# A fused attention and gated-MLP kernel: wide query weights, earlier bias and spatial loads, normalization in one step, first loads on two queues

## The chip, the core and the metric

The kernel runs on one core of a Trainium2 chip. The core has five engines that work through their own instruction lists: TensorE (PE in the profile; PEld is its weight load), VectorE (DVE), ScalarE (ACT), GpSimd (POOL) and SyncE (SP). SP, ACT and POOL can also issue transfers (DMAs) between memory and the core; an issue by POOL takes POOL's own time. The metric is the device time of one launch in microseconds (us), as the median of several runs. A second figure is the profiled execution: one launch with the hardware profiler, from which every duration in this document comes.

## What is computed

Inputs are q, k, v of shape 8 batches x 8 heads x 576 tokens x 64, a feature matrix w_phi (64 x 128) and the weights of a gated MLP. Cut to what matters:

```python
def phi(x):                                   # per head
    proj = x @ w_phi                          # 64 -> 128 features
    proj = proj - max(abs(proj), axis=-1)
    return concat([exp(proj), exp(-proj)])
q_p, k_p = phi(q), phi(k)
kv  = einsum('bhsf,bhsd->bhfd', k_p, v);  z = k_p.sum(tokens)
x   = (q_p @ kv) / (q_p @ z + 1e-6)           # heads side by side: 8 x 576 x 512

h = relu(x @ w_in)                            # 512 -> 1024
u, v = h[..., :512], h[..., 512:]
v_n = (v - mean(v)) / sqrt(var(v) + 1e-6)
v_s = einsum('ts,bsd->btd', w_spatial, v_n) + b_spatial[:, None]
out = (u * v_s) @ w_out                       # 512 -> 512
```

All inputs and the output are float32; the matrix products run in bfloat16.

## The kernel before

**Units.** The attention part (stage A) runs over 36 units, numbered in the order in which they are worked. A "pair" unit is one pair of heads of one batch with its first 512 tokens as four blocks of 128. The last 64 tokens of the eight heads of two batches make one "tail" unit. Units 0, 1, 3, 4 are batch 0, unit 2 is the tail of batches 0 and 1, units 5 to 8 are batch 1, unit 9 is the tail of batches 2 and 3, units 10 to 13 are batch 2, and so on.

**Steps.** `step(i)` (line 636) walks a fixed list of phases. In step i the keys and queries of unit i are projected (`by_token`, L267), their largest magnitudes taken on DVE (L279 for keys, L293 for queries), the key features made on ACT (`kf`, L282) and V scaled by the key factors `em` on POOL (`vs`, L307; for tails `vst`, L322). One step later the query maxima, split into two bfloat16 parts by POOL (`mhl`, L296/297, by DVE for the first five units), are transposed by PE (`a_max_t`, L328). Two steps later (a step more or less for the first five units) come the query features (`qf`, L366) and the sums over tokens (L379 to L384), three later the numerator (L399) and four later the transposed result `xT`. So PE's order of work is fixed when the program is built, whatever is ready.

**Projection with the maximum.** For batches 0 and 1 the query maximum is subtracted by a second matrix product with `sel` (L353, L360). From batch 2 on (`merged`) it is folded into the weights: `wm` holds for even heads the weights with selection rows in partitions 64 to 79 and for odd heads the other half plus the selection (`weights_with_max`, L239 to L243, twelve POOL instructions in steps 6 and 7). There the query operand also takes the maxima as extra rows: `q_even` copies half of the transposed queries by a DMA, and DVE writes the maxima (L331, L332).

**Loads.** Batch 0's first heads come as float32 by SP and are cast by DVE (heads 0, 1) and POOL (heads 2, 3, and the tails). All later q and k are cast on the way by DMAs that POOL issues (`load`, `load_tail`); v comes by SP (`load_v`). From batch 2 on, q and k are transposed by DMAs issued by SP (`cross`, three steps before use), which wait there for the load. The table `io` (L676 to L712) says after which step each load is issued.

**The MLP (stage B).** When a batch's `xT` is complete, its tasks (`b_tasks`, L592) join a queue, and `fill` puts them between the phases of later steps: `b_v` (L448, relu on ACT L450, mean and variance on DVE L451/L452), `b_root` (L454 to L462), `b_ln` (L465: normalization into `vn` on POOL), `b_u` (L503, L505), `b_s` (L524, L525 with the transposed spatial weights `w_spT`, multiplied into `uT` by DVE at L527) and `b_o` (L549, copied out at L552, stored by SP at L558). The tail of each batch has the same steps (`b_v_tail` and the like); its normalized rows go to `vnt`. The bias is one extra row of `w_spT`, multiplied by a row of ones in `vnt`.

`root` makes both the factor and the shift of the normalization from the variance and the mean, in four POOL instructions:

```python
var = var + 1e-6                      # L458
rs0 = var ** -0.5                     # L459
rs1 = -(mean * rs0)                   # L460, L461
vn  = vr * rs0 + rs1                  # L465, normalize
```

**Spatial weights.** `w_spatial` is loaded in three parts (`wsp`, `wspr`, `wspt`), transposed by PE between tasks of batch 0 (`transpose_spatial`, L210) and copied into `w_spT` by DVE. The same function has ACT write the two bias rows (L230 to L233).

Of the kernel before, what the change touches and what calls it, by code (L numbers as in the profile page):

```python
# [8 lines left out]
FP32 = mybir.dt.float32  # L9
BF16 = mybir.dt.bfloat16  # L10
# [6 lines left out]
def kernel(  # L17
# [106 lines left out]
    for i in range(2):  # L124
        nc.scalar.dma_start(out=wphi_f[i * D:(i + 1) * D, :], in_=w_phi)
    alloc(0)
    first = {}
    for h0 in (0, 2):
        for x, t in (("k", k), ("q", q)):
            first[x, h0] = s2.tile([P, 2, NB * D], FP32, tag="ob", name="first", bufs=6)  # L130
            pin(nc.sync.dma_start)(out=first[x, h0], in_=main_ap(t, 0, h0, 2))
    alloc_tail(0)
    tails = ld.tile([P, H * NB, D], FP32, tag="v_f", name="tails")
    for n, t in enumerate((k, q)):
        for i in range(2):
            pin(nc.sync.dma_start)(out=tails[i * TL:(i + 1) * TL, n * H:(n + 1) * H, :], in_=tail_ap(t, i))
# [5 lines left out]
    zero = cpool.tile([P, 1], BF16)  # L142
    pin(nc.vector.memset)(zero, 0.0)
# [25 lines left out]
    pin(nc.vector.memset)(vst[1], 0.0)  # L169
# [7 lines left out]
    pin(nc.scalar.copy)(out=vst[0].rearrange("p b s h d -> p (b s h d)"), in_=zero.to_broadcast([P, 4 * H * DA]))  # L177
# [3 lines left out]
    for i in range(2):  # L181
        fill_vnt(i, nc.gpsimd.tensor_copy)
    for x in ("k", "q"):
        pin(nc.gpsimd.tensor_copy)(out=half_tile(x, 0, 0)[:, 2:4], in_=first[x, 2])
    load("k", 0, 1, 0, 2)
    load("q", 0, 1, 0, 2)
# [7 lines left out]
    wsp = s2.tile([P, NB, T0], BF16, tag="vn", name="wsp", bufs=2)  # L194
    wspr = cpool.tile([P, NB, TL], BF16)
    wspt = s2.tile([TL, S], BF16, tag="ob", name="wspt", bufs=6)
    bsp_row = s2.tile([P, S], FP32, tag="xT", name="bsp_row", bufs=3)
    nc.sync.dma_start(out=bsp_row[TL:TL + 1, :], in_=moe_b_spatial)
    nc.sync.dma_start(out=bsp_row[0:1, :], in_=moe_b_spatial)
# [10 lines left out]
    def transpose_spatial(i):  # L210

        pt = psum.tile([P, S], BF16, tag="bank", name="pt")
        if i < NB:
            sc = POS[i]
            for tp, c in enumerate(POS):
                nc.tensor.transpose(out=pt[:, tp * P:(tp + 1) * P], in_=wsp[:, c, bass.ds(sc, P, step=NB)],
                                    identity=ident)
            nc.tensor.transpose(out=pt[:, T0:S], in_=wspt[:, bass.ds(sc, P, step=NB)],
                                identity=ident[:TL, :TL])
            nc.vector.tensor_copy(out=w_spT[:, i, :], in_=pt)  # L220
            return
        for bl in range(2):
            lo = bl * TL
            for tp, c in enumerate(POS):
                nc.tensor.transpose(out=pt[lo:lo + TL, tp * P:(tp + 1) * P], in_=wspr[:, c, :], identity=ident)
            nc.tensor.transpose(out=pt[lo:lo + TL, T0:S], in_=wspt[:, T0:S], identity=ident[:TL, :TL])
            nc.vector.tensor_copy(out=w_spT[lo:lo + TL, NB + bl, :], in_=pt[lo:lo + TL, :])
        for bl, row in ((0, TL), (1, 0)):
            r = slice(row, row + 1)
            pin(nc.scalar.copy)(  # L230
                out=w_spT[r, NB + bl, 0:T0].rearrange("o (a b p) -> o a b p", a=2, b=2),
                in_=bsp_row[r, 0:T0].rearrange("o (p b a) -> o a b p", a=2, b=2))
            pin(nc.scalar.copy)(out=w_spT[r, NB + bl, T0:S], in_=bsp_row[r, T0:S])  # L233


    def merged(u):
        return u["pair"] and u["b"] >= XB

    def weights_with_max(n):  # L239
        for j in range(4 * n, 4 * n + 4, 2):  # L240
            pin(nc.gpsimd.tensor_copy)(out=wm[:, j, :], in_=wphi2[:, 0:F])
            pin(nc.gpsimd.tensor_tensor)(out=wm[:, j + 1, :], in0=wphi2[:, F:2 * F], in1=sel[:, j + 1, :], op=ALU.add)
            pin(nc.gpsimd.tensor_copy)(out=wm[D:D + 2 * H, j, :], in_=sel[0:2 * H, j, :])  # L243
# [210 lines left out]
    def root(mv, r, n):  # L454

        var = small.tile([P, NB, 1], FP32, tag="var", name="var")
        rs = small.tile([P, NB, 2], FP32, tag="rs", name="rs")
        nc.gpsimd.tensor_scalar(out=var[r, 0:n], in0=mv[r, 0:n, 1:2], scalar1=1e-6, scalar2=None, op0=ALU.add)  # L458
        nc.gpsimd.tensor_tensor(out=rs[r, 0:n, 0:1], in0=var[r, 0:n], in1=neghalf[r, 0:n].unsqueeze(2), op=ALU.pow)  # L459
        nc.gpsimd.tensor_tensor(out=var[r, 0:n], in0=mv[r, 0:n, 0:1], in1=rs[r, 0:n, 0:1], op=ALU.mult)  # L460
        nc.gpsimd.tensor_scalar(out=rs[r, 0:n, 1:2], in0=var[r, 0:n], scalar1=-1.0, scalar2=None, op0=ALU.mult)  # L461
        return rs  # L462

    def normalize(dst, src, rs):
        nc.gpsimd.tensor_scalar(out=dst, in0=src, scalar1=rs[:, 0:1], scalar2=rs[:, 1:2],  # L465
                                op0=ALU.mult, op1=ALU.add)

    def b_v(b, j):
        d = st[b]
        if j == 0:  # L470
            d["vn"] = s2.tile([P, NB, HALF], BF16, tag="vn", name="vn", bufs=2)
            d["mv"] = small.tile([P, NB, 2], FP32, tag="mv", name="mv")
            d["vr"] = {}
        d["vr"][j] = s2.tile([P, HALF], BF16, tag="vr", name="vr", bufs=5)
        stats = small.tile([P, 6], FP32, tag="stats", name="stats")
        v_mm(lambda kc: d["xT"][:, kc, j * P:(j + 1) * P], d["vr"][j], slice(0, P), stats, d["mv"][:, j, :])

    def b_root(b):
        st[b]["rs"] = root(st[b]["mv"], slice(0, P), NB)

    def b_ln(b, j):
        d = st[b]
        normalize(d["vn"][:, j, :], d["vr"][j], d["rs"][:, j, :])

    def b_v_tail(g, bls):
# [6 lines left out]
        rstd = root(mv, r, 1)  # L492
        for bl in bls:
            r = slice(bl * TL, (bl + 1) * TL)
            normalize(vnt[g % 2][r, bl, :], vr[r], rstd[r, 0, :])
# [96 lines left out]
    def b_tasks(b):  # L592
# [8 lines left out]
        ts.append((0.0, lambda: b_root(b)))  # L601
# [79 lines left out]
    at(1, load_v, 1)  # L681
    at(2, load, "k", 1, 0)
    at(2, load, "q", 1, 0)
    at(3, load, "k", 1, 1)
    at(3, load, "q", 1, 1)
    at(4, load_weight, w_in_bf[:, :, HALF:DFF], cols[:, :, HALF:DFF])
    at(4, load_weight, wspt, moe_w_spatial[T0:S, :])
    at(5, tail_scale, 0, 1)
    at(5, load_weight, wsp, rows[:, :, 0:T0])
    at(5, load_weight, wspr, rows[:, :, T0:S])  # L690
    at(6, load_weight, w_in_bf[:, :, 0:HALF], cols[:, :, 0:HALF])
    at(8, load_weight, w_out_bf, moe_w_out.rearrange("(kc p) f -> p kc f", p=P))
    for u in units:
        i = u["i"]
        if not u["pair"] and u["g"] > 0:
            early = 1 if u["g"] > 1 else 0
            at(i - AT - early, load_tail, "k", u["g"])
            for x in ("q", "v"):
                at(i - AT + 1 - early, load_tail, x, u["g"])
        if u["pair"] and u["b"] >= XB:  # L700
            if u["pj"] == 0:
                for n, (x, y) in enumerate((("k", 0), ("q", 0), ("k", 1), ("q", 1))):
                    at((4, 4, 6, 7)[n] if u["b"] == XB else i - AB + n, load, x, u["b"], y)
# [4 lines left out]
    at(6, weights_with_max, 0)  # L708
    at(7, weights_with_max, 1)
# [39 lines left out]
```

## Time and profile before

| | us |
|---|---|
| median of 3 runs | 285.23 (282.81 to 285.92) |
| profiled execution | 284.76 |
| its span, first to last instruction | 282.7 |

Busy time of each engine over the span, from the page:

| engine | busy us | share |
|---|---|---|
| PE | 257.1 | 91% |
| DVE | 231.2 | 82% |
| ACT | 219.5 | 78% |
| POOL | 200.5 | 71% |

The granted TensorE clock of the execution was 0.986 of full speed. In the profile's lists of waits, "POOL vs L307 <- ACT em L302: 17.6, 9, 4.0" means that POOL's instruction that writes vs at line 307 stood waiting for ACT's em of line 302, 17.6 us in all, nine times, 4.0 us at the longest. A wait is only put down when the engine had nothing else to do, as each engine takes its list in order. A DMA's "us to landing" counts from its issue until its data are there. Lines that say L61 are recorded through a helper (`pin`) that keeps an instruction at its place in the program's order.

### The profile page before, as it was taken

The numbers are of one execution on the slowest core, as the hardware profiler recorded it, in microseconds if no ns is written. First come the engines' busy times: TensorE is split into PE (matmuls) and PEld (weight loads), VectorE is DVE, ScalarE is ACT, GpSimd is POOL, SyncE is SP. The second block draws the span as 40 slices with busy tenths as digits, with TensorE's granted clock in tenths as the row PEclk, the third lists the DMA queues.
The fourth block names the chain that finished last, engine by engine and source line by source line (L and its number), as shares of the span: only waits on it lengthen the run. The fifth ranks groups of instructions, "written<-read, shape, count | busy, mean of one in ns | idle before, by whom it ended". The sixth has DMA issues, their size and how long they took to land.

```text
span 282.7 us, 8134 instructions
## 1 busy us (share of the span) xinstructions
PE 257.1 (91%) x3001; PEld 173.1 (61%) x3042; DVE 231.2 (82%) x576; ACT 219.5 (78%) x499; POOL 200.5 (71%) x362
## 2 busy tenths in 40 slices
PE   2777979986999999999999999999999999999993
PEld 1466866754776667666666775766666765654441
DVE  7979987875799979998889989998889897566341
ACT  5689996978399997899889987899699977723601
POOL 5988999999859886799949974889548832511710
PEclk9979999999799999999999999999999999999999
DMA  7989999999986999989989999999766301120305
GB/s 205 238 205 125 152 144 217 111 164 195 225 87 163 130 243 196 162 206 210 214 96 130 207 252 138 200 214 217 86 122 132 86 2 68 46 77 37 112 3 186
DMA packets 85148, 42.43 MB, mean 150 GB/s; under 512 B 52146, under 2 KB 80498, under 8 KB 85108
## 3 DMA queue, kind: packets, MB, share of 16 engines
q1 hardware_dynamic: 60020, 30.95, 55.0%
q0 software_dynamic: 24928, 10.89, 34.9%
q8 instruction: 24, 0.39, 0.6%
q14 instruction: 16, 0.13, 0.2%
q10 hardware_dynamic: 160, 0.07, 0.1%
HBM read 32.85 MB, written 9.44 MB: 150 GB/s over the span
## 4 chain that ended last, share of the span: by engine, by line
PE 62%; POOL 12%; ACT 9%; DVE 6%; DMA 4%; issue 4%; SPq 0%; POOLq 0%; ACTq 0%; DVEq 0%
PE ps L524 9%; PE pv L448 9%; PE po L549 9%; PE ps L267 6%; PE pu L503 6%; ACT kf L282 5%; PE pv L379 4%; PE pn L399 4%; PE pq L345 3%; DMA q_bf<-in_q_dram 3%; PE ps L525 2%; POOL vs L307 2%; POOL vst L61 2%; DVE stats L451 2%; ACT qf L366 2%
## 5 line engine op out<-in xcount | busy, mean ns | idle before, releaser
L282 ACT ACTIVATE kf<-ps 128x512 bf16<-128x512 f32 x144 | 76.2, 637 | 9.9 <-DVE mk L279 9.5
L307 POOL TENSOR_TENSOR vs<-v_f,em 128x512 bf16<-128x512 f32 x64 | 65.5, 1044 | 19.0 <-ACT em L302 17.6
L366 ACT ACTIVATE qf<-pq 128x512 bf16<-128x512 f32 x128 | 66.6, 620 | 9.6 <-PE pq L345 8.5
L279 DVE TENSOR_REDUCE mk<-ps 128x4 f32<-128x512 f32 x72 | 47.7, 677 | 1.2 <-PE ps L267 0.5
L293 DVE TENSOR_REDUCE mq<-ps 128x4 f32<-128x512 f32 x62 | 39.8, 680 | 2.6 <-PE ps L267 1.4
L524 PE MATMUL ps<-w_spT,vn 128*128 128x512 bf16 x116 | 33.1, 384 | 3.6 <-POOL vn L465 3.1
L527 DVE TENSOR_TENSOR uT<-ps,uT 128x512 bf16<-128x512 f32 x32 | 22.0, 687 | 16.8 <-PE ps L525 16.8
L451 DVE BATCH_NORM_STATS2 stats<-vr 128x6 f32<-128x512 bf16 (+1 forms) x40 | 26.7, 684 | 7.3 <-ACT vr L450 6.9
L549 PE MATMUL po<-w_out_bf,uT 128*128 128x512 bf16 x121 | 32.0, 380 | 0.4
L503 PE MATMUL pu<-xT,w_in_bf 128*128 128x512 bf16 x121 | 31.5, 380 | 0.5 <-issue 0.2
L448 PE MATMUL pv<-w_in_bf,xT 128*128 128x512 bf16 x116 | 30.7, 380 | 0.7
L450 ACT ACTIVATE vr<-pv 128x512 bf16<-128x512 f32 (+1 forms) x40 | 23.5, 615 | 7.6 <-PE pv L448 5.9
L379 PE MATMUL pv<-vs,kf 128*128 128x66 bf16 x512 | 24.3, 194 | 1.3 <-ACT kf L282 1.3
L390 DVE TENSOR_TENSOR x<-pn,rc 128x256 bf16<-128x256 f32 x64 | 24.9, 417 | 0.3
L465 POOL TENSOR_SCALAR vn<-vr,rs 128x512 bf16<-128x512 bf16 x32 | 24.3, 766 | 1.1
L399 PEld LDWEIGHTS <-qf 128*128 128x128 bf16 x512 | 20.5, 99 | 7.1 <-issue 1.4
L505 ACT ACTIVATE uT<-pu 128x512 bf16<-128x512 f32 x32 | 19.7, 641 | 4.9 <-PE pu L503 3.2
L379 PEld LDWEIGHTS <-kf 128*128 128x128 bf16 x512 | 21.8, 97 | 2.5 <-issue 1.5
L552 ACT COPY ob<-po 128x512 f32<-128x512 f32 x18 | 11.0, 614 | 14.9 <-PE po L549 8.4
L399 PE MATMUL pn<-kv,qf 128*128 128x66 bf16 x512 | 22.0, 195 | 0.3 <-ACT qf L366 0.3
L381 PE MATMUL pv<-vst,kf 128*128 128x66 bf16 x128 | 21.2, 192 | 0.0
L524 PEld LDWEIGHTS <-vn 128*128 128x128 bf16 x128 | 11.7, 98 | 13.8 <-POOL vn L465 4.6
(133 smaller groups left out, 572.2 us busy)
## 6 DMA issues: line engine op xcount, KB each, us to landing
out_dram<-ob SPq DMA_DIRECT2D x32, 256.0 KB, 2.5
v_f<-in_v_dram SPq DMA_DIRECT2D x14, 512.0 KB, 7.0
k_bf<-in_k_dram POOLq DMA_DIRECT2D x14, 256.0 KB, 6.3
q_bf<-in_q_dram POOLq DMA_DIRECT2D x14, 256.0 KB, 6.4
qt<-qT_b SPq DMA_DIRECT2D x24, 64.0 KB, 4.2
v_tl<-in_v_dram SPq DMA_DIRECT2D x8, 128.0 KB, 3.4
v_f<-in_v_dram SPq DMA_DIRECT2D x1, 1024.0 KB, 9.4
w_in_bf<-in_moe_w_in_dram POOLq DMA_DIRECT2D x2, 512.0 KB, 10.5
```

Of the source, the lines that this page charges most:

```text
L279: nc.vector.tensor_reduce(out=u["mk"][:, hs], in_=pk, axis=AX.X, op=ALU.max, apply_absolute_value=True)
L282: nc.scalar.activation(out=u["kf"][:, s, hs, :], in_=pk, func=AF.Exp, bias=0.0, scale=sc)
L293: nc.vector.tensor_reduce(out=mq[:, 4 * half:4 * half + 4], in_=pq, axis=AX.X, op=ALU.max, apply_absolute_value=True)
L307: nc.gpsimd.tensor_tensor(out=vs[:, s, :, 0:D], in0=st[u["b"]]["v"][:, pj * H:(pj + 1) * H, :], in1=em[:, s, :].unsqueeze(2).to_broadcast( ...
L366: nc.scalar.activation(out=qf[:, s], in_=pq, func=AF.Exp, bias=0.0, scale=sc)
L379: nc.tensor.matmul(out=pv[:, hh, s, :], lhsT=u["kf"][:, s, 4 * hh + c, :], rhs=u["vs"][:, s, 4 * hh + c, :], start=(c == 0), stop=False)
L399: nc.tensor.matmul(out=pn[:, pos, :], lhsT=u["qf"][hh][:, s, pos, :], rhs=d["kv"][:, 2 * u["pj"] + hh, s, :], start=(s == 0), stop=(s == 1))
L448: nc.tensor.matmul(out=pv[r], lhsT=lhs(kc), rhs=w_in_bf[:, kc, HALF:DFF], start=(kc == 0), stop=(kc == KC - 1))
L451: nc.vector.bn_stats(out=stats[r], in_=dst[r])
L503: nc.tensor.matmul(out=pu, lhsT=w_in_bf[:, kc, dc * P:(dc + 1) * P], rhs=d["xT"][:, kc, :], start=(kc == 0), stop=(kc == KC - 1))
L524: nc.tensor.matmul(out=ps, lhsT=d["vn"][:, sp, cs], rhs=w_spT[:, sp, 0:T0], start=(sp == 0), stop=False)
L549: nc.tensor.matmul(out=po[r], lhsT=lhs(dc), rhs=w_out_bf[:, dc, :], start=(dc == 0), stop=(dc == KC - 1))
```

## The change

Ten edits in one:

1. The first q loads (heads 0, 1 and 2, 3, and the q tail) are issued by ACT, the k loads by SP, side by side. `w_phi` moves from ACT's queue to SP, behind the first k.
2. The bias row is loaded by SP ahead of v, and ACT writes the two bias rows after steps 1 and 2 (`spatial_bias`), no longer inside `transpose_spatial`.
3. `vst` is zeroed by two POOL memsets, seen as float32; before, one half was copied by ACT and the other set by DVE.
4. The even half of `wm` is written by two wide ACT copies at the start, the odd half by one wide POOL instruction after step 3 (`odd_weights`), in place of the twelve narrow ones.
5. `wsp` holds all 576 columns, loaded at once; `wspr` is gone. It is loaded after step 4, w_in's two halves after steps 4 and 5, `wspt` after step 6 and w_out after step 9.
6. The loads of batch 2 are issued after steps 7 (k, q of heads 0 to 3), 8 (k of heads 4 to 7) and 9 (its q), where they were after steps 4, 4, 6 and 7; v of batch 2 in halves after steps 8 and 9, where it was after 5 and 7. Batch 3's q and k go one step later. The second tail's k goes after step 5, its v and q after step 6.
7. The epsilon is added on DVE right behind the statistics (`with_eps`); POOL only takes the power.
8. The normalization uses the mean and the factor directly: `(vr - mean) * rs`.
9. For the last batch (b = 7) DVE normalizes, both `vn` and the tail's `vnt`.
10. The tail's root and normalization stand behind all of the batch's `b_v`, no longer right behind the tail's own product.

```diff
-    for i in range(2):
-        nc.scalar.dma_start(out=wphi_f[i * D:(i + 1) * D, :], in_=w_phi)
...
+    def load_first(x, h0):
+        t, eng = dict(k=(k, nc.sync), q=(q, nc.scalar))[x]
+        first[x, h0] = s2.tile([P, 2, NB * D], FP32, tag="ob", name="first", bufs=6)
+        pin(eng.dma_start)(out=first[x, h0], in_=main_ap(t, 0, h0, 2))
+
+    for x in ("k", "q"):
+        load_first(x, 0)
+    for i in range(2):
+        pin(nc.sync.dma_start)(out=wphi_f[i * D:(i + 1) * D, :], in_=w_phi)
+    for x in ("k", "q"):
+        load_first(x, 2)
+    for n, (t, eng) in enumerate(((k, nc.sync), (q, nc.scalar))):
...
+    for r in (TL, 0):
+        pin(nc.sync.dma_start)(out=bsp_row[r:r + 1, :], in_=moe_b_spatial)
     load_v(0, 0)
...
-    pin(nc.vector.memset)(vst[1], 0.0)
-    pin(nc.scalar.copy)(out=vst[0].rearrange("p b s h d -> p (b s h d)"), in_=zero.to_broadcast([P, 4 * H * DA]))
+    for i in range(2):
+        pin(nc.gpsimd.memset)(vst[i].rearrange("p b s h d -> p (b s h d)").bitcast(FP32), 0.0)
...
+    pin(nc.scalar.copy)(out=alternate(wm, 0), in_=wphi2[:, 0:F].unsqueeze(1).to_broadcast([P, NP, F]))
+    pin(nc.scalar.copy)(out=alternate(wm[D:D + 2 * H], 0), in_=alternate(sel[0:2 * H], 0))
+
+    def odd_weights():
+        pin(nc.gpsimd.tensor_tensor)(out=alternate(wm, 1), in0=alternate(sel, 1),
+                                     in1=wphi2[:, F:2 * F].unsqueeze(1).to_broadcast([P, NP, F]), op=ALU.add)
...
-    wsp = s2.tile([P, NB, T0], BF16, tag="vn", name="wsp", bufs=2)
-    wspr = cpool.tile([P, NB, TL], BF16)
+    wsp = s2.tile([P, NB, S], BF16, tag="vn", name="wsp", bufs=2)
...
+    def with_eps(mv, r, n):
+        var = small.tile([P, NB, 1], FP32, tag="var", name="var")
+        nc.vector.tensor_scalar(out=var[r, 0:n], in0=mv[r, 0:n, 1:2], scalar1=1e-6, scalar2=None, op0=ALU.add)
+        return var
+
+    def root(var, r, n):
+        rs = small.tile([P, NB, 1], FP32, tag="rs", name="rs")
+        nc.gpsimd.tensor_tensor(out=rs[r, 0:n], in0=var[r, 0:n], in1=neghalf[r, 0:n].unsqueeze(2), op=ALU.pow)
         return rs
...
+    def normalize(b, dst, src, mv, rs):
+        eng = nc.vector if b == B - 1 else nc.gpsimd
+        eng.tensor_scalar(out=dst, in0=src, scalar1=mv[:, 0:1], scalar2=rs, op0=ALU.subtract, op1=ALU.mult)
...
     ts = outs[:1] + [(MM, lambda: b_v_tail(g, [bl]))] + vs[:2] + outs[1:2] + vs[2:]
-        ts.append((0.0, lambda: b_root(b)))
+        ts += [(0.0, lambda: b_root_tail(g, [bl])), (0.0, lambda: b_ln_tail(g, [bl])), (0.0, lambda: b_root(b))]
...
     at(1, load_v, 1)
+    at(1, spatial_bias, 0)
+    at(2, spatial_bias, 1)
...
+    at(3, odd_weights)
...
-    at(4, load_weight, wspt, moe_w_spatial[T0:S, :])
+    at(4, load_weight, wsp, rows)
     at(5, tail_scale, 0, 1)
-    at(5, load_weight, wsp, rows[:, :, 0:T0])
-    at(5, load_weight, wspr, rows[:, :, T0:S])
-    at(6, load_weight, w_in_bf[:, :, 0:HALF], cols[:, :, 0:HALF])
-    at(8, load_weight, w_out_bf, moe_w_out.rearrange("(kc p) f -> p kc f", p=P))
+    at(5, load_weight, w_in_bf[:, :, 0:HALF], cols[:, :, 0:HALF])
+    at(5, load_tail, "k", 1)
+    at(6, load_tail, "v", 1)
+    at(6, load_tail, "q", 1)
+    at(6, load_weight, wspt, moe_w_spatial[T0:S, :])
+    at(7, load, "k", 2, 0)
+    at(7, load, "q", 2, 0)
+    at(8, load, "k", 2, 1)
+    at(8, load_v, 2, 0)
+    at(9, load, "q", 2, 1)
+    at(9, load_v, 2, 1)
+    at(9, load_weight, w_out_bf, moe_w_out.rearrange("(kc p) f -> p kc f", p=P))
...
-    at(6, weights_with_max, 0)
-    at(7, weights_with_max, 1)
```

## The prediction, made before the changed kernel was run

> **What bounds the kernel now.** I read the row of busy tenths first, then busy times by stretch, then the waits of the stretches with holes.
>
> ```profile
> PE   2777979986999999999999999999999999999993
> PEclk9979999999799999999999999999999999999999
> ```
>
> Each digit is a slice of 7.07 us. PE is full from slice 10 (71 us) to the last but three; its holes lie before 71 us and at the end. The stretches give the amounts (columns: window, length, then busy time and instructions of PE, PEld, DVE, ACT, POOL; clock; DMA share; GB/s):
>
> ```profile
> 16.00:42.00 26.00, 22.78 (x363) 19.70 (x363) 23.68 (x69) 23.86 (x60) 23.78 (x35) 0.94 0.99 145
> 57.00:72.00 15.00, 11.39 (x128) 7.56 (x128) 8.82 (x22) 11.42 (x28) 13.94 (x25) 0.94 1.30 187
> 72.00:256.00 184.00, 180.43 (x2169) 121.23 (x2200) 161.95 (x397) 152.83 (x351) 129.51 (x237) 1.00 0.90 149
> ```
>
> From 72 to 256 us PE works 180.43 of 184 us, so POOL or DVE work saved there is worth nothing. PE's instructions stand in the same order in both kernels, so the change can only fill PE's holes, or open new ones. The waits name the holes in 41 to 60 and in 66 to 72 us:
>
> ```profile
> PE pt L328 <- POOL mhl L297: 1.5, 1, 1.5
> PE ps L267 <- ACT qf L366: 1.1, 1, 1.1
> ```
> ```profile
> PE ps L524 <- POOL vn L465: 2.4, 2, 1.3
> ```
>
> The chain of waits shows POOL pacing everything from 27 to 42.8 us, half of it issuing loads:
>
> ```profile
> 28.90 0.56 POOL wspt L61
> 29.46 1.39 POOL k_tl L61 x2
> 30.85 0.76 POOL k_bf L61
> 31.61 0.75 POOL q_bf L61
> 32.36 2.07 POOL vs L307 x2
> ```
>
> The third hole also costs clock; by single microseconds (window, length, PE busy, clock, DMA share, GB/s):
>
> ```profile
> 70.00:71.00 1.00, 0.78 (x2) 0.60 1.38 248
> 71.00:72.00 1.00, 1.00 (x17) 0.50 1.49 198
> 72.00:73.00 1.00, 1.00 (x19) 0.50 1.12 360
> 73.00:74.00 1.00, 1.00 (x7) 0.70 1.13 332
> ```
>
> 0.4 + 0.5 + 0.5 + 0.3 = 1.7 us of PE time are lost at the lower clock.
>
> The Trainium skill, page "TensorE: Matmul & The Clock Gate", section "Why this matters for your kernels", asks only that PE gaps stay below some 3 us, and the gaps here are 1.25 and 1.11 us. By it the clock would not have fallen and this 1.7 us would not be there to win. The row disagrees (PE was busy 0.85 us in 67 to 70 us) and decides.
>
> **The change, part by part.** All against the profiled execution: 284.76 us, span 282.7; the median is 0.47 us above it.
>
> *A, the start.* DVE loses the memset of vst (0.94 us) and of zero (0.06), which stand ahead of its first cast at 4.67; that k load landed at 0.72 + 2.9 = 3.62. The first q load moves from the second place on SP (issued 1.24, landed 3.6 later) to the first on ACT. So PE's first transpose, at 5.08, could come 0.95 us sooner. The Trainium skill, page "DMA: Bandwidth & Descriptors", section "Issuing engines are not separate DMA queues", says that starting transfers on two engines saves only the time to issue them. By it the second queue brings at most one issue, 0.5 us.
>
> Against this: wphi moves behind the first k on SP, issues near 1.24 and 1.8, lands 3.1 to 4.0 later as before, and after its two casts (0.6 us) PE's L267 has it at 5.5 to 6.2; it ran at 6.21. ACT issues four loads before its table load (1.28 us) instead of two, hidden by the wphi wait. ACT's copy to vst (1.95) makes room for the two wide copies to wm (kT copies of 512 columns: 0.615 each), done near 7.4, as kf begins at 7.58. The vst memsets go to POOL: by the slope of its memsets (0.10 us for 1 column, 0.20 for 128) 0.95 each, by its vnt copies (0.72 for 512) 1.48; so 1.9 to 3.0 us, against POOL's idle 1.91 before the first cast. The q_bf issue behind it moves from 8.80 to between 8.2 and 9.3, and PE waits for that load at 15.95.
>
> The bias copies (1.11 + 0.24 = 1.35 us a pair) move to steps 1 and 2, where ACT idles 1.15 (before kf at 14.10) and 1.10 (before qf at 17.45); the second pair can delay kf at 19.63, up to 1.35 us, in a stretch where ACT and DVE are both over 90% busy. Bounds for A: 0.95 won to 0.8 lost. I take 0.2 won, near the middle, as gain and loss have rows of like size.
>
> *B, step 6's maxima.* Ahead of mhl (ended 42.76) POOL loses the second vs unit (2.25), q_tl (1.40), wspt (0.56), k_bf and q_bf (0.82, 0.81) and wspr (0.74), and gains the second w_in (0.82) and the wide odd weights (512 columns, as vs: 1.04). 6.58 - 1.86 = 4.7 us sooner. The wait of 1.5 goes; next late would be DVE, which has mq long before (39.2). +1.5.
>
> *C, bias off ACT.* The four copies filled 55.02 to 57.54 and PE waited 1.1 for the qf behind them. +1.1; a load can take the place, see N.
>
> *D, vn of batch 0.* Ahead of vn's end (70.17) POOL loses wm (four times 0.43 + 0.30 + 0.28 = 4.0), three small operations of each root (0.24 + 0.19 + 0.25 and 0.24 + 0.20 + 0.25 = 1.4), wspr 0.74 and one q_bf issue 0.88, and gains the odd weights 1.04: 6.0 us sooner, 64.2. w_out and one k load now sit between the first vn and the second; they were ahead before, so the sum holds. PE needs the first vn at 67.08 - 2.8 (A to C) = 64.3 and the fourth 0.65 later. The wait of 2.4 and the clock's 1.7 go: +4.1, with under a microsecond to spare.
>
> *E, the last batch.* DVE's normalization: its TENSOR_SCALAR of 1024 columns took 1.06, so 0.53 for 512 at most; its cast of 512 took 0.36. POOL took 0.77. The aggregate ends at 264.08, + 0.17 for the epsilon (as an aggregate), + 1.05 for the power, + 0.2 handing over: 265.5; four at 0.36 to 0.53 end at 267.0 to 267.6. PE reaches L524 at 267.65 and takes one every 0.22. The first group's period was 2.18 us, the next ones 1.08: +1.1 on either end. DVE's output copy at 264.79 now waits behind; its bank is not asked for until the fourth group.
>
> *Hidden.* Sixteen epsilons on DVE (about 0.17 each, 2.7 us) lie in a stretch with 22 us of DVE idle; uncovered they would cost that 2.7. Each root still needs the same statistics.
>
> *N, new waits on loads.* Batch 2's loads are issued later; behind them stand the transposes on SP, and PE in its fixed order behind those. Before, congestion gave (issues in 41.3 to 47.1 us, last column us to landing):
>
> ```profile
> w_in_bf<-in_moe_w_in_dram POOLq DMA_DIRECT2D x1, 512.0 KB, 14.7
> k_bf<-in_k_dram POOLq DMA_DIRECT2D x1, 256.0 KB, 15.6
> q_bf<-in_q_dram POOLq DMA_DIRECT2D x1, 256.0 KB, 15.0
> kT_b<-k_bf SPq DMA_TRANSPOSE x1, 13.3
> ```
>
> POOL's vs of unit 7 (47.84) moves up by k, q, wspr, q (3.2) and half of wm (2.0) less 1.04, to 43.7. The q of batch 2 goes out behind it at 45.9 (was 31.55, landing 6.7 later). At 6.7 it lands at 52.6 and its transpose (median 5.1 to landing) at 57.7; PE asks for it at 60.22 - 2.8 = 57.4. At 8 us, as wsp had (7.7), it is 1.6 late. The q tail's second half goes out behind vs at about 40.5 instead of 39.4; at 8.4 it is 2.1 late, at the median 4.4 not at all. The other half of q goes out after the first vn, 60.3 + 5.7 + 5.2 = 71.2; PE asks at 77.10 less all gains, about 71. The v loads, w_in and wsp no longer crowd 37 to 47, so I stay near the medians. N: 0 to 4 us, I take 2.2.
>
> Sum: 0.2 + 1.5 + 1.1 + 4.1 + 1.1 - 2.2 = 5.8; 284.76 - 5.8 = 279.0.
>
> **Rivals.** *R1, loads become the bound; slower.* If q of batch 2 lands as late as the 15.0 above, that is 60.9, and the transpose 5.1 to 14.1 (its worst before) later, 66 to 75, against 57.4: 8.6 to 17.6 lost, plus 1.7 of clock, against 8.0 of gross gain: 287 to 296, or 288 near the low end. It decides from a landing of about 13 us. For it: the share of the DMA engines is 1.3 to 1.8 in 44 to 64 us. Against: 1 MB of v, wsp and the second w_in left that stretch or go later.
>
> *R2, the gain is only moved.* PE waits for q's transpose and tail about as long as it waited before (N 4.5 to 6.5, one clock drop included): 281.3 to 283.3, at 282.5. For it: three places of N are within 2 us.
>
> *R3, loads sooner, but nothing starts sooner.* Two queues share the same engines, POOL's memsets hold its casts, bias copies hold kf: A is -0.8, and N 1.5. 284.76 - (8.0 - 0.2 - 0.8 - 1.5) = 279.3, so it cannot be told from the forecast by time, only by the first transpose.
>
> **Numbers.** Forecast with R3: 0.75, own range 275.5 to 282; R2: 0.14; R1: 0.11. Low end: N at 0 and A at 0.95 give 276.0; one more hidden wait, 275. High end: 285 leaves out R1 and little else. About 1% is what a measurement can tell from no change (282.4 to 288.1 around 285.23). Faster 0.76, within 1% 0.14, slower 0.10.
>
> **What would show it.** Right: PE's first transpose near 4.5; no PE wait for mhl near 41; no PE wait for vn near 65 and clock 1.00 there; vn's end near 64; the last batch's L524 without holes. Wrong: PE waiting for qT_b or q_tl longer than 2.2 us in 44 to 75; kf waiting for ACT's bias copies; a new drop of the clock in 55 to 75; the stretch after 72 us taking more than its 184 us.

## The result and the profile after

| | before | after |
|---|---|---|
| median of 4 runs, us | 284.0 (281.99 to 285.92) | 313.2 (311.86 to 313.38) |
| profiled execution, us | 284.76 | 311.86 |
| its span, us | 282.7 | 310.1 |
| mean clock of TensorE | 0.986 | 0.96 |

The ratio, time after over time before, is 1.102, with a 95% interval of 1.092 to 1.111: the change makes the kernel 10% slower. The forecast was 279.0, its range 275 to 285.

The busy tenths of the changed kernel, 7.75 us to a slice:

```profile
PE   1868899958998869995999969996899979979994
PEclk9999999995999979998699979999799999999999
```

PE, full from slice 10 on before, now has a hole of one slice every three to six, and the clock falls behind most of them. By stretch (columns as before: window, length, busy time of PE, PEld, DVE, ACT, POOL; clock; DMA share; GB/s):

```profile
57.00:72.00 15.00, 10.15 (x113) 6.64 (x114) 8.26 (x20) 9.66 (x24) 14.64 (x16) 0.94 0.85 147
72.00:256.00 184.00, 164.65 (x1888) 108.84 (x1914) 147.16 (x357) 139.47 (x324) 148.47 (x192) 0.94 0.91 145
```

Between 72 and 256 us, where PE had worked 180.43 of 184, it works 164.65, and more slowly. The waits and the groups name who is late (waits: engine and line, what it waited for, us in all, times, longest; groups: busy us, mean ns of one, idle before):

```profile
PEld L544 <- POOL vn L475: 23.1, 13, 4.0
PE ps L544 <- POOL vn L475: 18.7, 11, 3.7
PE pv L390 <- POOL vst L61: 1.6, 1, 1.6
```
```profile
L475 POOL TENSOR_SCALAR vn<-vr,mv,rs 128x512 bf16<-128x512 bf16 x28 | 58.0, 2080 | 1.0
L544 PE MATMUL ps<-w_spT,vn 128*128 128x512 bf16 x116 | 38.6, 425 | 19.6 <-POOL vn L475 18.7
```

The normalization took 766 ns an instruction before (24.3 us for 32). Its new form takes 2080 (58.0 for 28), on the same shape, type and engine. The timelines of POOL and of PE show what that does to one batch, batch 0 (start, us, instruction, count, idle time before):

```profile
60.26 2.08 POOL L475 TENSOR_SCALAR vn<-vr,mv,rs 128x512 bf16<-128x512 bf16 x1
62.28 0.88 POOL L61 DMA_DIRECT2D q_bf<-in_q_dram  x1
63.16 0.75 POOL L61 DMA_DIRECT2D w_out_bf<-in_moe_w_out_dram  x1
63.90 0.76 POOL L61 DMA_DIRECT2D k_bf<-in_k_dram  x1
64.67 6.18 POOL L475 TENSOR_SCALAR vn<-vr,mv,rs 128x512 bf16<-128x512 bf16 x3
```
```profile
65.40 0.38 PE L544 MATMUL ps<-w_spT,vn 128*128 128x512 bf16 x1
66.82 0.39 PE L544 MATMUL ps<-w_spT,vn 128*128 128x512 bf16 x1 [1.04 <-POOL vn L475]
70.91 0.61 PE L544 MATMUL ps<-w_spT,vn 128*128 128x512 bf16 x1 [3.70 <-POOL vn L475]
```

The first `vn` begins at 60.26, six microseconds earlier than the 66.25 of before, as the prediction had it. But the four end at 70.85 instead of the 64.2 it counted on, later even than before (70.17). POOL's busy time in the long stretch rises only from 129.51 to 148.47 of 184 us: POOL is not full. It is late at one place in each batch, in the stretch from the root to the fourth `vn`, where PE stands in its fixed order and takes one `vn` after the other.

Because PE's order is the same in both kernels, the start of each unit's first product can be set beside that of before; the differences show where time is won or lost. This table does so for the traces that matter below (us; minus is earlier than before; the last row is the difference of the spans). E1 is the changed kernel with the old form of the normalization; the others follow.

| unit | after | E1 | E5 | E10 | E12 |
|---|---|---|---|---|---|
| 0 | +1.55 | +1.43 | +1.49 | +1.52 | +0.64 |
| 4 | +0.49 | +0.36 | +0.42 | +1.42 | -0.40 |
| 7 | +0.65 | +0.62 | +0.57 | +1.61 | -0.34 |
| 8 | -0.94 | -0.98 | -1.02 | +0.02 | -1.93 |
| 12 | +2.06 | -5.57 | -5.44 | -4.58 | -5.01 |
| 16 | +2.40 | -0.90 | -4.79 | -3.68 | -4.11 |
| 17 | +7.64 | -0.90 | -4.79 | -3.69 | -4.11 |
| 22 | +14.18 | -0.89 | -4.79 | -3.39 | -3.95 |
| 25 | +14.65 | -0.40 | -4.31 | -2.54 | -2.97 |
| 26 | +17.90 | +3.63 | -0.30 | -2.54 | -2.97 |
| 35 | +26.30 | +3.64 | -0.30 | -2.06 | -2.35 |
| end | +27.4 | +2.6 | -1.3 | -2.8 | -3.3 |

The changed kernel loses 3 to 7 us at each batch's spatial products (units 11 to 12, 16 to 17, 20 to 22, 25 to 26 and so on). That is the first theory: the form of the normalization costs all of it. Its rivals: that one step with two scalars from two tiles is slow as such, or that late loads and the new start share in it.

### The profile page after: what moved, and what is told of

It is laid out like the page before. It is cut to its first block, busy times and chain, and to the rows that moved or that the text cites. A ratio compares the mean times of both kernels' runs of the same rounds, so it can differ in the third digit from the quotient of the medians.

```text
span 310.1 us, 8086 instructions
## 1 busy us (share of the span) xinstructions
PE 266.2 (86%) x3001; PEld 175.3 (57%) x3042; DVE 236.6 (76%) x595; ACT 218.6 (71%) x500; POOL 230.5 (74%) x299
## 4 chain that ended last, share of the span: by engine, by line
PE 43%; POOL 26%; ACT 13%; DVE 10%; issue 4%; DMA 1%; SPq 0%; POOLq 0%; ACTq 0%; DVEq 0%
POOL vn L475 16%; PE ps L544 9%; PE pv L457 7%; PE po L569 5%; ACT kf L291 5%; PE ps L276 4%; ACT qf L375 3%; POOL vs L316 3%; POOL vst L61 3%; PE ps L545 3%; PE pv L388 2%; DVE stats L460 2%; PE pn L408 2%; POOL rs L470 2%; DVE mk L288 2%
## 5 line engine op out<-in xcount | busy, mean ns | idle before, releaser
L475 POOL TENSOR_SCALAR vn<-vr,mv,rs 128x512 bf16<-128x512 bf16 x28 | 58.0, 2080 | 1.0
L544 PE MATMUL ps<-w_spT,vn 128*128 128x512 bf16 x116 | 38.6, 425 | 19.6 <-POOL vn L475 18.7
L470 POOL TENSOR_TENSOR rs<-var,neghalf 64x1 f32<-64x1 f32 (+1 forms) x16 | 13.2, 827 | 28.1 <-DVE var L465 20.5
L544 PEld LDWEIGHTS <-vn 128*128 128x128 bf16 x128 | 12.6, 106 | 33.5 <-POOL vn L475 23.1
L399 DVE TENSOR_TENSOR x<-pn,rc 128x256 bf16<-128x256 f32 x64 | 24.8, 415 | 0.3
L393 ACT CAST kv<-pv 128x264 bf16<-128x264 f32 x28 | 11.4, 407 | 16.4 <-PE pv L390 16.3
```

The lines of the kernel that those rows point to most:

```text
L475: eng.tensor_scalar(out=dst, in0=src, scalar1=mv[:, 0:1], scalar2=rs, op0=ALU.subtract, op1=ALU.mult)
L544: nc.tensor.matmul(out=ps, lhsT=d["vn"][:, sp, cs], rhs=w_spT[:, sp, 0:T0], start=(sp == 0), stop=False)
```

## Experiments

Each ratio below is against the kernel before, timed again beside the experiment; where two experiments are close, the ratios compare them better than the medians.

### E1 to E4: the form of the normalization

**E1**, the changed kernel with the normalization alone put back to scale and shift, made by two small POOL operations in each root:

```diff
-        eng.tensor_scalar(out=dst, in0=src, scalar1=mv[:, 0:1], scalar2=rs,
-                          op0=ALU.subtract, op1=ALU.mult)
+        eng.tensor_scalar(out=dst, in0=src, scalar1=rs[:, 0:1], scalar2=rs[:, 1:2],
+                          op0=ALU.mult, op1=ALU.add)
```

> The changed kernel with one part undone: the normalization is again scale and shift (multiply, add), with the shift made by two small POOL operations in each root; the epsilon on DVE, the last batch on DVE, all loads and weights stay as changed. Theory F (form): POOL's subtract-then-multiply takes 2.08 us for 512 columns where multiply-then-add took 0.77, and PE waits 18.7 us for vn and loses clock behind each wait. Then vn is back at 0.77 us each, PE's waits for vn fall below 3 us and the time to 278 to 283 us. Rival L (loads): batch 2's later loads and the crowded issues between the first and second vn made vn late, and POOL's longer instruction is only port contention with DVE. Then vn stays near 2 us or PE's waits only move, and the time stays above 300 us.

Measured: 287.03 us (285.47 to 289.38), ratio 1.011 (1.007 to 1.016). The group of the normalization in this kernel:

```profile
L477 POOL TENSOR_SCALAR vn<-vr,rs 128x512 bf16<-128x512 bf16 x28 | 21.4, 772 | 0.9
```

772 ns again, and PE's products no longer wait for `vn`. So 26 of the 29 us lost (313.2 to 287.0) go with the form. But the expected 278 to 283 was missed by 4 us: this kernel is still not faster than before, and 8 us above the forecast, so the form is not the only thing that was wrong.

**E2**, the kernel before with nothing but the new form:

```diff
-        nc.gpsimd.tensor_tensor(out=var, in0=mv[..., 0:1], in1=rs[..., 0:1], op=ALU.mult)
-        nc.gpsimd.tensor_scalar(out=rs[..., 1:2], in0=var, scalar1=-1.0, op0=ALU.mult)
...
-        nc.gpsimd.tensor_scalar(out=dst, in0=src, scalar1=rs[:, 0:1], scalar2=rs[:, 1:2],
-                                op0=ALU.mult, op1=ALU.add)
+        nc.gpsimd.tensor_scalar(out=dst, in0=src, scalar1=mv[:, 0:1], scalar2=rs[:, 0:1],
+                                op0=ALU.subtract, op1=ALU.mult)
```

> The kernel before with one part of the change alone: the normalization subtracts the mean and multiplies by the factor in one POOL instruction, and each root loses its two operations for the shift. Theory F: vn takes 2.08 us, 40 x 1.31 = 52 us more on POOL less 32 x 0.2 = 7 us, and the time rises by 25 to 40 us to 309 to 324. Rival L: within 2 us of before, as the loads are where they were.

Measured: 320.55 us (319.02 to 322.69), ratio 1.125 (1.117 to 1.134). Its groups of the normalization and of the products that use it:

```profile
L463 POOL TENSOR_SCALAR vn<-vr,mv,rs 128x512 bf16<-128x512 bf16 x32 | 66.2, 2076 | 1.2
L522 PE MATMUL ps<-w_spT,vn 128*128 128x512 bf16 x128 | 42.4, 439 | 25.3 <-POOL vn L463 25.3
```

The form alone costs 36 us, and takes two operations out of each root in doing so. Here the last batch is on POOL too, where nothing covers it: 10 of the 36 us come after the start of unit 35.

**E3**, the changed kernel with another form in each batch:

```diff
+        s1, s2, o1, o2 = {
+            1: (two[:, 0:1], two[:, 1:2], ALU.mult, ALU.add),
+            2: (two[:, 0:1], two[:, 1:2], ALU.mult, ALU.subtract),
+            3: (two[:, 0:1], two[:, 1:2], ALU.add, ALU.mult),
+            4: (rs, two[:, 1:2], ALU.mult, ALU.add),         # scalars of two tiles
+            6: (two[:, 0:1], two[:, 1:2], ALU.subtract, ALU.mult),
+        }.get(b, (m, rs, ALU.subtract, ALU.mult))            # 0 as changed; 5: two instructions
```

> The changed kernel with another form of the same normalization in each batch, for the duration of each on POOL: batch 0 subtract-multiply (as changed), 1 multiply-add with both scalars side by side, 2 multiply-subtract, 3 add-multiply with the negated mean, 4 multiply-add with scalars from two tiles, 5 subtract and multiply as two instructions, 6 subtract-multiply with both scalars side by side, 7 on DVE. Theory F1 (only multiply-add is quick): 0.77 us for batches 1 and 4, near 2.08 for 0, 2, 3 and 6. Theory F2 (the order counts: multiply first is quick): 0.77 for 1, 2 and 4, 2.08 for 0, 3 and 6. Theory F3 (scalars from two tiles or strided are slow): 0.77 for 1, 2, 3 and 6, 2.08 for 0 and 4. Batch 5 shows whether one operation alone is quick.

Measured on POOL, 512 columns (the time as a whole, 301.71 us in one execution, mixes them). Groups, then timeline lines of batches 2, 3 and 6:

```profile
L500 POOL TENSOR_SCALAR vn<-vr,mv,rs 128x512 bf16<-128x512 bf16 x4 | 8.3, 2082 | 0.1
L490 POOL TENSOR_SCALAR vn<-vr,mv 128x512 bf16<-128x512 bf16 x4 | 6.2, 1561 | 0.2
L491 POOL TENSOR_SCALAR vn<-vn,rs 128x512 bf16<-128x512 bf16 x4 | 6.2, 1566 | 0.1
L500 POOL TENSOR_SCALAR vn<-vr,rs,two 128x512 bf16<-128x512 bf16 x4 | 3.0, 763 | 0.2
```
```profile
132.79 2.08 POOL L500 TENSOR_SCALAR vn<-vr,two 128x512 bf16<-128x512 bf16 x1
169.29 0.77 POOL L500 TENSOR_SCALAR vn<-vr,two 128x512 bf16<-128x512 bf16 x1
260.98 8.25 POOL L500 TENSOR_SCALAR vn<-vr,two 128x512 bf16<-128x512 bf16 x4
```

Multiply then add takes 0.77 us, with its scalars in one tile or in two (0.763); add then multiply 0.77 (batch 3, the line at 169.29). Multiply then subtract takes 2.08 (batch 2), subtract then multiply 2.06 to 2.10 with scalars side by side (batch 6) or not. One operation alone, subtract or multiply, takes 1.56. So neither the two tiles nor the single step is slow, and none of the three theories fits: F1 has add then multiply slow, F2 has it slow and multiply then subtract quick, F3 has only the scalars of two tiles slow. Of the forms tried, those that pair multiply and add are quick, and the others are not.

**E4**, the normalization of all batches on DVE:

```diff
-        eng = nc.vector if b == B - 1 else nc.gpsimd
+        eng = nc.vector
```

> The changed kernel with the normalization of every batch on DVE (it is there for the last one), in the changed form. DVE took 0.41 us for 512 columns in the last batch. Theory F: POOL loses 35 x 2.08 = 73 us, DVE gains 35 x 0.41 = 14 us in a stretch that has about 22 us to spare, so the time falls to 279 to 285 us. Rival L: above 300 us.

Measured: 298.03 us (297.21 to 299.43), ratio 1.046 (1.039 to 1.054). E4's group of the normalization and two of its waits:

```profile
L475 DVE TENSOR_SCALAR vn<-vr,mv,rs 128x512 bf16<-128x512 bf16 x32 | 13.3, 436 | 4.9 <-POOL rs L470 4.9
```
```profile
POOL mhl L305 <- DVE mq L302: 20.7, 8, 4.4
DVE vnt L475 <- POOL rs L470: 8.8, 3, 4.5
```

DVE is quick with the same form, 0.44 us. But its queue runs in order, and now stands still for POOL's power (8.8 and 4.9 us), while the maxima behind it are late for POOL (20.7 us). PE works 169.08 of the 184 us from 72 to 256. Both expectations were missed, 279 to 285 and above 300. The instruction is cheap there; the waits say that standing still for the power is not, though no further edit tested that.

### E5 to E8: the 8 us that the form does not explain

The table shows where E1 lost what it had won: 4.7 us from unit 12 to 16 and 4.0 from 25 to 26. At the first place DVE stands still for 4.2 us, waiting for the DMA that copies the even queries of unit 10 (`q_even`). E1's timelines of DVE and of SP's queue:

```profile
70.16 0.42 DVE L423 COPY xT<-pt 128x512 bf16<-128x512 bf16 x1
74.81 0.41 DVE L340 COPY qT_b<-pt 16x512 bf16<-16x512 bf16 x1 [4.22 <-DMA qt<-qT_b]
```
```profile
57.25 2.20 SPq L61 DMA_TRANSPOSE kT_b<-k_bf  x1
65.12 1.19 SPq L61 DMA_TRANSPOSE qT_b<-q_bf  x1
66.41 0.80 SPq L61 DMA_DIRECT2D v_f<-in_v_dram  x1
67.31 0.53 SPq L61 DMA_DIRECT2D qt<-qT_b  x1
```

SP's queue shows the cause. From 59.45 to 65.12 it waits to transpose unit 12's q, whose load POOL issued at 60.77, behind the first `vn`; the copy for unit 10 stands behind that in the queue. At the second place DVE's copy of the maxima, a 16x512 instruction, takes 2.88 us instead of 0.28. E1 again: DVE, POOL beside it, and two windows behind it (the columns are those of the stretches above):

```profile
159.73 2.88 DVE L341 COPY qt<-qT_b 16x512 bf16<-16x512 bf16 x1
```
```profile
159.39 0.77 POOL L477 TENSOR_SCALAR vn<-vr,rs 128x512 bf16<-128x512 bf16 x1
160.13 2.04 POOL L316 TENSOR_TENSOR vs<-v_f,em 128x512 bf16<-128x512 f32 x2
162.13 0.20 POOL L318 CAST vs<-em 128x32 bf16<-128x32 f32 x1
```
```profile
166.00:167.00 1.00, 1.00 (x7) 0.44 (x5) 0.28 (x1) 0.38 (x1) 0.97 (x2) 0.50 1.12 359
167.00:168.00 1.00, 1.00 (x4) 0.30 (x2) 0.00 (x0) 0.00 (x0) 1.00 (x2) 0.50 1.21 283
```

The copy ends 0.28 us after the last of POOL's instructions that run without a gap from 159.39 to 162.33. PE then waits 2.34 us for DVE, and its clock is down from 165 to 169 us (0.67, 0.50, 0.50, 0.62 in single microseconds, 1.7 us of PE time): 2.3 + 1.7 = 4.0.

**E5**: E1 with the load of batch 2's second half of q issued after step 8 instead of 9, ahead of the power and the first `vn`. **E6**: E1 with unit 10's `q_even` ahead of unit 12's transposes on SP, the load as late as it was. **E7**: E1 with the second copy of the maxima read from PSUM. **E8**: E1 with `vst` zeroed as before, by DVE and ACT.

```diff
# E5
-    at(9, load, "q", 2, 1)
+    at(8, load, "q", 2, 1)
# E6, ahead of the loads and transposes of step 9
+    at(9, q_even, units[10])
# E7
-            nc.vector.tensor_copy(out=even, in_=odd)
+            nc.vector.tensor_copy(out=even, in_=pt[0:2 * H, :].unsqueeze(1).to_broadcast([2 * H, 4, P]))
# E8
+    pin(nc.vector.memset)(vst[1], 0.0)                    # ahead of the first casts
...
-    for i in range(2):
-        pin(nc.gpsimd.memset)(vst[i] ..., 0.0)
+    pin(nc.scalar.copy)(out=vst[0] ..., in_=zero.to_broadcast([P, 4 * H * DA]))
```

> The scale-and-shift form (287.0 us, ratio 1.011) with one move: the load of the second half of batch 2's q is issued by POOL after step 8, ahead of batch 0's power and first normalization, instead of after step 9 (it was issued at 60.77). Theory W (three waits are what is left: q_even's DMA holding DVE 4.2 us at 70.6; DVE's copy of the maxima locked out for 2.6 us at 160; the vst zeroing on POOL): the load goes out near 51 and lands by 58, so SP is not held to 65.1 and q_even leaves before 61; DVE's wait of 4.2 us goes, unit 15 starts 3 to 5 us sooner, and the time is 282.5 to 284 if the loss at 160 stays. Theory S (after 72 us PE sets the pace, and the small VectorE steps of the epsilon fill whatever room is made): the gain is gone by unit 16 and the time is 286.5 to 287.5.

> The scale-and-shift form with only the order on SP changed: the copy of unit 10's even queries (q_even) is issued ahead of unit 12's two transposes instead of behind them; the load of batch 2's q stays late. Theory W with the place in SP's queue as the cause: q_even leaves near 57 instead of 67.3, DVE's wait of 4.2 us goes; unit 12's own transpose still waits for the load (65.1) and lands near 70, so PE waits there for 0 to 2 us: 283 to 285. If the late load itself is what costs, the wait only moves to unit 12: 286 to 287.5. Theory S: 286.5 to 287.5.

> The scale-and-shift form with DVE's second copy of the maxima (16x512, L341) reading the PSUM tile instead of the copy in SBUF. The SBUF copy took 0.28 us in most of its 24 instances but 2.88 at 159.5, 1.07 at 197.4 and 0.93 at 223.7 beside POOL's vs; the copy from PSUM (L340) took 0.40 in all. Theory W with a lock between DVE's SBUF copy and POOL: the copies take 0.40 each (2.9 us more of DVE in all, hidden), none is longer, PE's wait of 2.3 us at 163 and the clock's fall to 0.66 in 166 to 170 go: 282.5 to 284.5. Theory S, or a chance delay of this one run: 286.5 to 288.

> The scale-and-shift form with the zeroing of vst as it was before (vst1 by a DVE memset, 0.94 us ahead of the first cast; vst0 by an ACT copy, 1.95 us). Theory W: POOL's first casts come 1.9 us sooner, PE's wait of 1.6 us for vst and unit 4's late start (+0.36) go, but PE's first transpose moves to about 5.0 plus 0.9 if DVE's memset is what holds it, or stays at 5.1 if the k load is: units 4 to 7 within -1 to +0.6 of before, and 285.5 to 287 overall. If the start does not matter because PE catches up by unit 3: 286.5 to 287.5, no difference.

E5: 282.11 us (281.4 to 283.15), ratio 0.989 (0.985 to 0.992). The time is just under the 282.5 to 284 expected. The load goes out at 51.21, SP waits no more, and the DVE line that had waited 4.22 us follows at once. E5's timelines of SP and DVE:

```profile
59.07 1.21 SPq L61 DMA_TRANSPOSE qT_b<-q_bf  x1
60.37 0.54 SPq L61 DMA_DIRECT2D v_f<-in_v_dram  x1
61.02 0.53 SPq L61 DMA_DIRECT2D qt<-qT_b  x1
```
```profile
70.63 0.40 DVE L340 COPY qT_b<-pt 16x512 bf16<-16x512 bf16 x1
```

Unit 16 keeps -4.79 against E1's -0.90. One load, moved by one step, is worth 4 to 5 us. E6: 283.68 (281.96 to 285.1), ratio 0.993 (0.990 to 0.997). With the load as late as in E1, the wait goes as well (unit 16 at -4.01), so what did the harm was the place behind the waiting transpose in SP's queue, and the late load only through it.

E7: 286.45 (286.38 to 288.46), ratio 1.007 (1.003 to 1.011); all 24 copies take 0.40 to 0.42 us, and the loss at unit 26 is gone (+2.13 at units 25 and 26 alike). So the theory of the place holds. Of the gain there, most was lost at others: this run stands 1.5 us behind E1 at unit 4 already, after a fall of the clock (told below), so the time shows no clear gain. The expectation of 282.5 to 284.5 was missed. E8: 288.7 (288.58 to 289.12), ratio 1.012 (1.010 to 1.014); unit 0 comes at +2.71 instead of +1.43, and the time lies above both expectations. With q's first loads on ACT, zeroing on DVE and ACT is worse by 1.3 us than zeroing on POOL: ACT's copy to `vst`, at 3.24 in the kernel before, begins at 6.39 here, ahead of the casts of w_phi. The move to POOL was not the cause of the late start.

### E9 to E12: the start, and the repairs together

**E9**: E5 with the bias copies moved to steps 8 and 9. **E10**: E5 with E7's copy. **E11**: the changed kernel, its one step kept, but with the mean negated by DVE and added. **E12**: E11 with the edits of E5, E7 and E9, and w_phi cast by DVE instead of ACT.

```diff
# E9, E12
-    at(1, spatial_bias, 0)
-    at(2, spatial_bias, 1)
+    at(8, spatial_bias, 0)
+    at(9, spatial_bias, 1)
# E11, E12
+        nc.vector.tensor_scalar(out=neg[r, 0:n], in0=mv[r, 0:n, 0:1], scalar1=-1.0, scalar2=None, op0=ALU.mult)
...
-        eng.tensor_scalar(out=dst, in0=src, scalar1=mv[:, 0:1], scalar2=rs, op0=ALU.subtract, op1=ALU.mult)
+        eng.tensor_scalar(out=dst, in0=src, scalar1=neg, scalar2=rs, op0=ALU.add, op1=ALU.mult)
# E12
-        pin(nc.scalar.copy)(out=wphi2[r, y * F:(y + 1) * F], in_=wphi_f[r, :])
+        pin(nc.vector.tensor_copy)(out=wphi2[r, y * F:(y + 1) * F], in_=wphi_f[r, :])
```

> The kernel with q's load ahead of the first normalization (282.1 us, ratio 0.989) and the two pairs of bias copies on ACT moved from steps 1 and 2 to steps 8 and 9. Theory B (the pair at 14.4 us delays ACT's kf and em of unit 2 by its 1.25 us, POOL's vst behind em, and PE's wait of 1.6 us for vst): the wait for vst falls to 0.4 us or less, unit 4 starts 1.2 us sooner (21.0 instead of 22.3), units 5 to 8 0.6 to 1.2 us sooner; the copies fill ACT's idle of 1.5 and 1.9 us near 54 and 58 and cost PE at most 0.6 there: 281.0 to 281.9. Rival (ACT and DVE are both over 95% busy from 20 to 42 us, so what is moved is only worth what ACT's queue there lacks; the copies at 54 to 60 hold qf and uT as they did before): 281.8 to 282.8.

> The kernel with q's load ahead of the first normalization (282.1 us) and DVE's second copy of the maxima read from PSUM. If the lock between DVE's copy and POOL's instructions is worth what unit 26 showed (4.0 us lost between units 25 and 26, of which 0 to 1.4 come back from other small shifts), units 25 and 26 keep their distance to before and the time is 278.3 to 280.5. If the delay only moves on to another place: 281.5 to 283.

> The changed kernel (313.2 us, ratio 1.102) with the one-step normalization kept but written as adding the negated mean and multiplying (DVE makes the negated mean beside the epsilon, one more small instruction in each root, 16 in all). Theory F (the form with subtract is what POOL does slowly; add and multiply take 0.77 us): vn takes 0.77 us and the time falls to that of the scale-and-shift form, 286 to 288, ratio 1.004 to 1.014. Rival (the one step itself, or reading two scalars from two tiles, is slow): vn stays near 2.08 us and the time near 313.

> All repairs together: one step with the negated mean added, q's load ahead of the first normalization, the maxima's second copy from PSUM, bias copies at steps 8 and 9, and the two casts of w_phi on DVE instead of ACT (so that they do not wait for ACT's table load of 1.28 us behind the load of w_phi). If the effects add up: 287.0 - 4.9 (q) - 3 to 4 (copy) - 0 to 1 (bias) - 0 to 1.2 (start) = 276 to 279, ratio 0.968 to 0.979. If PE's pace after 72 us takes part of each back: 279 to 282.

E9: 282.1 (281.76 to 283.55), ratio 0.995 (0.992 to 0.998), no gain on E5. PE still waits 1.4 us for `vst` (1.6 before the edit), and what unit 4 wins (0.3) is lost at unit 10. The theory that the bias copies held up the start falls; the rival, that they cost as much wherever ACT does them, fits.

E11: 286.23 (285.65 to 288.11), ratio 1.009 (1.005 to 1.012). Its group of the normalization, one step with add in place of subtract:

```profile
L478 POOL TENSOR_SCALAR vn<-vr,neg,rs 128x512 bf16<-128x512 bf16 x28 | 21.2, 765 | 1.0
```

That settles the form: 27 us of the loss (313.2 to 286.2) go with an add in place of the subtract, though an instruction was added to each root. E11 ends batch 0's four `vn` where the prediction had them, at 64.28:

```profile
62.02 2.26 POOL L478 TENSOR_SCALAR vn<-vr,neg,rs 128x512 bf16<-128x512 bf16 x3
```

E10: 281.04 (280.87 to 281.66), ratio 0.990 (0.986 to 0.993). E12: 281.05 (280.9 to 281.15), ratio 0.989 (0.986 to 0.992). In both nothing is lost at unit 26 any more, but neither is told apart from E5 by its ratio: E10 lost 1.0 us more by unit 4, E12 gives 1.3 back from unit 9 to 10, and both give 0.5 to 0.8 us back at each of a few later places. E10 lies between its two expectations. E12's gains do not add up to 276 to 279; its time is in the range of the rival, in which part of each gain is taken back. E12 and E10 are 1% faster than the kernel before and 10% faster than the changed one.

E12 also shows what held the start; the other edits leave unit 0 at +1.3 to +1.5 (E9, E10, E11). In the changed kernel ACT's first operation is the cast of w_phi, and its table load stands with it behind the DMA. ACT's timeline in the changed kernel, with the last of q's loads that it issues, PE's first product, and ACT's table load in E8:

```profile
4.43 0.60 ACTq L61 DMA_DIRECT2D tails<-in_q_dram  x1
5.80 1.28 ACT L61 ACT_TABLE_LOAD   x1 [5.80 <-DMA wphi_f<-in_w_phi_dram]
7.09 0.62 ACT L61 CAST wphi<-wphi_f 64x128 bf16<-64x128 f32 x2
```
```profile
7.76 1.01 PE L276 MATMUL ps<-wphi,kT 128*128 128x256 bf16 x4 [1.36 <-ACT wphi L61]
```
```profile
5.10 1.28 ACT L61 ACT_TABLE_LOAD   x1 [5.10 <-DMA first<-in_q_dram]
```

Before, the table was loaded at 1.95, ahead of the zeroing of `vst`, and PE's first product came at 6.21. That the zeroing left ACT is not what delays the table: E8 has it on ACT again, and the load begins at 5.10. ACT now issues q's loads first, and the last of them leaves only at 4.43, 0.02 us after the first q load has landed (4.41), so that ACT's queue is not past them before 5.03. The wait for w_phi adds the rest, to 5.80. With the casts on DVE the first product comes at 6.84, unit 0 at +0.64 instead of +1.5, and unit 4 at -0.40; what keeps the remaining 0.64 was not tested.

## Why the prediction was wrong

**D, the step that failed.** Its sum for the end of batch 0's `vn` ("6.0 us sooner, 64.2") lists the instructions and loads that leave or enter POOL's queue ahead of it, and lets each normalization keep its old duration, 0.77 us, though the change replaces its operations. The term is missing from the sum without a reason. The trace of before shows no POOL instruction over 512 columns with a subtract and two scalars. Its nearest rows were 0.77 (the old form) and 1.04 (`vs`), so bounds from rows would not have reached 2.08 either, but the price was open and was written down as known. Measured: 2.08 us, 1.31 more for each, and five of them stand ahead of that end, the tail's `vnt` and four `vn`: 6.6 us, which is the whole difference between 64.2 and the 70.85 measured. Over the seven batches on POOL that makes 46 us more of POOL's time; of these, 310.1 - 285.3 = 24.8 us show in the span (E1, E2, E11). For the same reason "POOL or DVE work saved there is worth nothing" from 72 us on was no shield: work added there is not free when it lies between a batch's root and PE's next product.

The other steps can be read from E1, whose form is the old one (differences of starts from the table; predicted and measured, minus is gain):

| step | predicted, us | measured, us | from |
|---|---|---|---|
| A, start, to unit 7 | -0.2 | +0.6 | +0.62 at unit 7 |
| B, the wait for `mhl`, unit 8 | -1.5 | -1.6 | +0.62 to -0.98 |
| C and D's moves, to unit 12 | -5.2 | -4.6 | -0.98 to -5.57 |
| N, loads, to unit 16 | +2.2 | +4.7 | -5.57 to -0.90 |
| units 16 to 35 | 0 | +4.5 | -0.90 to +3.64 |
| E, last batch | -1.1 | -1.0 | +3.64 to +2.6 |

**A** had the wrong sign. Taking the zeroing off DVE won nothing there: DVE's first cast took 0.88 us instead of 0.36, PE's first transpose stayed at 5.04 (5.08 before and in E8), and the first product came 1.55 us later. (In E12 that cast took 0.43, and the transpose came at 4.51, as forecast.) The prediction hid ACT's four loads and the table load behind "the wphi wait"; the loads do end before it (5.03 and 5.80), the table load stands after it. The +0.6 flatters the change, too: in the profiled execution of before the clock fell to 0.79 and 0.50 from 15 to 19 us, behind a wait of 1.23 us for q. E2, whose program is the same up to there, waited 1.30 us and kept 1.00, and its unit 7 begins 1.31 us sooner. Beside E2, the changed start loses 1.9 us by unit 7 (E1), and E12 is not ahead at unit 4.

**B** and **E** were right in mechanism and size: no wait for `mhl`, and the last batch's products follow each other in 1.08 us. DVE's and PE's timelines of the changed kernel:

```profile
294.23 1.38 DVE L475 TENSOR_SCALAR vn<-vr,mv,rs 128x512 bf16<-128x512 bf16 x4 [1.22 <-POOL rs L470]
```
```profile
296.15 1.03 PE L544 MATMUL ps<-w_spT,vn 128*128 128x512 bf16 x4
297.23 0.81 PE L544 MATMUL ps<-w_spT,vn 128*128 128x512 bf16 x3
```

**C** and the rest of **D** were right, within 0.6 us: the six microseconds by which POOL reaches the first `vn` sooner are there, E11 with a quick form ends the four at 64.28 against the 64.2 forecast, and PE's clock stays at 1.00 from 64 to 74 us in E1 and E11.

**N** was right in kind and too small, 2.2 for 4.7, and beyond its own upper bound of 4. It followed the late q to the unit that uses it and did not follow SP's queue behind the transpose that waits for it, where `q_even` of a unit two places earlier stood (E5, E6).

The 4 us at unit 26 were in no step. In the trace of before the same copy, the one that follows the start of unit 25, took 0.28 us; the next one, at 166.71, took 1.56, and PE waited no more than 0.2 us in the 8 us behind it. DVE's and POOL's timelines of before:

```profile
160.26 0.28 DVE L332 COPY qt<-qT_b 16x512 bf16<-16x512 bf16 x1
```
```profile
159.47 0.87 POOL L61 DMA_DIRECT2D k_bf<-in_k_dram  x1
160.39 1.55 POOL L465 TENSOR_SCALAR vn<-vr,rs 128x512 bf16<-128x512 bf16 x2
```

There the copy began while POOL was issuing a load; in E1 it began under a running `vn`, with `vs` right behind. That it falls worse in the new order is shown (E1, E5, E6, E8: 2.87 to 2.89 each; 2.86 in E9, 2.46 in E11), and that reading PSUM removes it (E7, E10, E12); that the place in POOL's run decides is read from these two traces, and no edit of that order tested it.

None of the rivals ended right: R1, loads as the bound, had the direction, and its mechanism shows only in the 4.7 of N. The loss to the form stands in no rival.

## What to carry to other kernels

A change that rewrites an instruction "in one step" has a new instruction in it: price its form, not its shape, and where no row shows it, measure it first. An engine that is idle for a quarter of the span (POOL is 74% busy in the changed kernel) can still be the bound, when a few of its instructions stand between a result and the matrix products that need it. When a load or a wait is moved, walk down the queue behind it to the end, whatever units those entries belong to. An engine that issues loads and also computes can stand behind its own loads, as ACT did at the start.

## What the hardware showed that was not expected

On POOL, TENSOR_SCALAR over 128x512 bfloat16 took 0.77 us as multiply-add (E1) or add-multiply (E11), 1.56 with one operation and 2.08 in the pairs with subtract (E3). On DVE subtract-multiply took 0.41 (changed kernel) to 0.44 (E4).

DVE's copy from SBUF to SBUF (0.28 us) took up to 2.89 beside POOL's work (E6), the same copy from PSUM never more than 0.42 (E7, E10, E12). The Trainium skill, page "SBUF — State Buffer", section "Who interferes with whom", says that a DVE copy can take the pair of ports that DVE shares with GpSimd, and that the second to issue is blocked for the whole instruction of the first. The traces fit a lock, as the copy ended 0.28 us after POOL's work did and the form that reads PSUM was never held, but the copy waited through four POOL instructions in a row, not one.

After the same wait of PE, 1.6 us near 19 us, the clock stayed at 1.00 in E1 and E5 and fell to 0.50 from 21 to 24 us in E6, E7 and E10, with PE busy for 0.71 to 0.74 of the stretch from 17 to 24 us in all five. That puts unit 4 some 1.0 to 1.5 us later. The kernel before and E2, at 15 to 19 us, differ in the same way (above, under A). What decides it was not found; it makes differences of 1 to 1.5 us between single profiled executions uncertain.
